# Attention and a squared-ReLU MLP on one core: an h pair ahead of each o stage, weight sums with their tiles taken together

## The chip, the cores and the metric

One core of one Trainium2 chip runs the whole program. Its engines are PE (TensorE, matrix products into PSUM), DVE (VectorE), ACT (ScalarE), POOL (GpSimd) and SP (SyncE, which here only issues transfers). Each engine works through its own queue in order. The time is that of one execution on the device, in microseconds (us); several runs are taken and their median is compared.

## The reference

Causal attention in float32, then an MLP on its output:

```python
# q, k, v: (4, 12, 448, 64); q and k are scaled up by 8
scores = q @ k.transpose / sqrt(64); scores = where(mask, -1e9, scores)
attn = exp(scores - max); attn = attn / (sum + 1e-9)
x = (attn @ v).transpose(0, 2, 1, 3).reshape(1792, 768)
h = maximum(x @ w_in, 0)          # w_in (768, 2048)
out = h * h @ w_out               # w_out (2048, 768); float32 out
```

## The kernel before

**Two halves.** The 1792 tokens are taken in two halves of 896 (two batches each). The first half (up to about 402 us) runs attention for all heads and the MLP of the first 896 tokens. The second half runs the MLP of the other 896 tokens, and this is the part that the change rearranges. Every float32 operand of a product is split into a high part (rounded, type float32r) and a low part (the rest); a product is three matmuls (high x high, high x low, low x high).

**Seven products for eight.** In the second half each 2 x 2 block product is done with seven products of sums of blocks (Strassen's scheme, in Winograd's form); `SEVEN` lists them as 11, 12, s3, s1, s2, 22, s4. The 2048 hidden columns are worked in four groups of 512, in the order `TURNS` = 0, 3, 2, 1. A group `gr` has

- two h pairs (`h_pair`, u = 0 and 1; each 21 products, matmul lines L797, L799, L801). A pair accumulates in four PSUM banks; ACT and DVE move banks into y tiles (pool r, and f_0 to f_2 of late memory), add, apply ReLU and square, and `factor` splits seven results into g7 tiles (high part on POOL or ACT, low part on DVE, line L300). There are 12 g7 tiles (g_92 to g_95, two in each, and g_0 to g_3).
- an o stage (`o_seven`, for the last group `o_last`; 42 or 48 products, lines L922 to L924). Each bank is added into a sum in SBUF (sa, sb) by DVE, or copied by ACT in the first group; some banks are accumulated on again after that.

**Weights of the second half.** A product needs a w tile with both parts; there are nine (eight in `wi`, one named w). Three of the seven can come ready split from DRAM (`wi_split`, lines L737; `wo_split`, L897), which was written in the first half. The sums of weight blocks (s1 to s4) are made by `added_up`: SP loads a block (L672) into an f tile, POOL or ACT negates or copies it (L690, L297), and POOL issues transfers that load another block and add it to the tile (L678). `done` then splits the result into a w tile. Groups 2 and 1 split the plain blocks too (`kept` is false). f tiles: eleven in the `words` buffer of the first half and one in late memory (f_3), shared by the sums (kind oz, up to 12), the x parts (xp), group 0's sums (fz) and the output (tr).

**What sets the order.** Nothing is ordered by hand: each step is an op with a rank (its due time), one or more engines that can do it, and what these cost. `Plan.emit` takes, again and again, the op that can start earliest by these costs (the lower rank where equal), gives it an engine and tiles, and so writes each engine's queue. `w_parts`, `o_parts` and `added_up` give the weight work ranks ahead of its stage by `LEAD` and the numbers in `added_up`; `ahead` and `begun` keep one set of weights behind the one before. `x_part` loads and splits 21 x parts (L660) at the end of the first half.

Of the kernel before, what the change touches and what calls it, by code (L numbers as in the profile page):

```python
# [17 lines left out]
PE, ACT, DVE, POOL, DMA, DMA2 = range(6)  # L18
# [153 lines left out]
def kernel(  # L172
# [17 lines left out]
    nc = tc.nc  # L190
# [35 lines left out]
    TURNS, LEAD = (0, 3, 2, 1), 9  # L226
# [40 lines left out]
    plan.pool("f", [], fz=5, xp=3, oz=12, tr=3)  # L267
# [395 lines left out]
    ahead, begun = [], []  # L663

    def added_up(rank, n, source, done, shaped, kept):

        def loaded(key, at):
            h = Hold("f", "oz")  # L670
            src, saved = source(key)
            plan.op(at, [(DMA, 0.7, lambda: nc.sync.dma_start(out=shaped(h.t[:, :n]), in_=src))],  # L672
                    saved, [h], begun, take=h)
            return h

        def added(h, key, at):
            src, saved = source(key)
            plan.op(at, [(POOL, 1.1, lambda: nc.gpsimd.dma_start(  # L678
                out=shaped(h.t[:, :n]), in_=src, accum_op=ALU.add))], saved, [h])
            plan.op(at, [(DMA, 0.7, lambda: None)], [], [h])  # L680

        def derived(a, scale, h=None, at=0.0, drop=()):
            to, take = (h, None) if h else (Hold("f", "oz"),) * 2

            def dst():
                return to.t[:, :n]

            def src():
                return a.t[:, :n]
            plan.op(at, [(POOL, t_pool(n), lambda: nc.gpsimd.tensor_scalar(  # L690
                dst(), src(), scale, 1.0, op0=ALU.mult, op1=ALU.mult)),
                on_act(n, dst, src, scale=scale)], [a], [to], take=take, drop=drop)
            return to
# [12 lines left out]
        done("s2", b)  # L706
        added(d, "12", rank - 4)
        done("s4", d)
        if not kept:
            done("12", loaded("12", rank - 5))  # L710
            done("22", loaded("22", rank - 3))

    def w_parts(gr, u, rank, last):
# [48 lines left out]
        if gr == 0:  # L762
# [6 lines left out]
            begun[:] = plan.ops[-2:]  # L769
# [14 lines left out]

    def h_pair(u, W, rank, step, plain):

        bank = {k: Hold("ps", "st") for k in "abcd"}
        y = {k: Hold("r", "y") for k in ("u2", "u3", "11", "12", "21")}
        f1, f2 = 2 * u, 2 * u + 1
# [81 lines left out]
        factor("t4", "21", True)  # L871
        return rank
# [7 lines left out]
    g7, sums = {}, {}  # L880
# [49 lines left out]
    def o_seven(gr, W, rank, step):  # L930

        bank = {}
        for key in SEVEN:
            b, k, begin = O_BANK[key], O_SUM[key], key not in ("12", "22", "s4")
            for d in range(CB):
# [3 lines left out]
                rank = o_product(ps, [(W[key, u], g7[OTHER[key], u]) for u in range(2)], d, begin, True, rank, step)  # L939
# [19 lines left out]
    def o_last(W, rank, step):  # L959

        for k in ("11", "21", "12", "22"):
            i, j = k
            for d in range(CB):
                ps, a = Hold("ps", "os"), o_sum(k, d)
                rank = o_product(ps, [(W[i + m, u], g7[m + j, u]) for m in "12" for u in range(2)],
# [68 lines left out]
    def group(ph, gr, rank, step, begin):  # L1034

        if ph == 0:
            for c in range(NP):
                at = begin + (rank - begin) * (c + 0.5) / NP
                piece(at, "i", gr, c, 0, ())
                if gr in (0, NG - 1):  # L1040
                    keep(at + 4, gr, c, swap)
        else:
            us = 7 * CB * H_US * step
            W = [w_parts(gr, u, rank + u * us - LEAD, rank + (u + 1) * us - LEAD) for u in range(2)]
        begin = rank
        if ph == 0 and gr == 0:
# [5 lines left out]
        elif ph == 0:  # L1052
# [3 lines left out]
        else:  # L1056
            for u in range(2):
                rank = h_pair(u, W[u], rank, H_US * step, gr == TURNS[-1])
        if ph == 0:
            for i in range(2 * GF):  # L1060
                at = begin + (rank - begin) * (i + 0.5) / 8
                piece(at, "o", gr, i % GF, i // GF, swap)
            begin = rank
            for ch in range(2):
                for t in range(NT):
                    rank = o_unit(gr, t, ch, rank, O_US * step, swap)
        else:
            begin = rank
            W = o_parts(gr, rank - LEAD, rank + 42 * H_US * step - LEAD)
            rank = o_last(W, rank, H_US * step) if gr == TURNS[-1] else o_seven(gr, W, rank, H_US * step)  # L1070
# [4 lines left out]
    for gr in range(NG):  # L1075
        begin, rank = group(0, gr, rank, (rest + NA * 7.0) / rest, begin)
# [68 lines left out]
```

## Time and profile before

| | |
|---|---|
| median of 3 runs | 628.52 us (626.83 to 628.68) |
| profiled execution | 631.88 us, its span 630.1 us |
| PE busy | 596.7 us, 95% of the span |
| DVE, ACT, POOL busy | 429.3, 358.6, 380.4 us (68%, 57%, 60%) |
| bytes moved | 120.01 MB, mean 190 GB/s |

The profile is of one execution. Busy time is the time in which an engine has an instruction under way; a matmul's duration is longer than its spacing, since matmuls overlap. Times within the span are counted from its start. "Idle before" an instruction is ascribed to what released it. The granted clock is the share of full speed that TensorE's clock was given; 1.00 is 2.4 GHz and 0.50 is 1.2 GHz.

### The profile page before, as it was taken

What the parts mean: (1) busy time and instruction counts of PE and PEld (TensorE: products, weight loads), DVE (VectorE), ACT (ScalarE), POOL (GpSimd) and SP (SyncE); (2) the same over time, 40 slices, a digit from 0 to 9 for tenths busy, and PEclk for the clock granted to TensorE, in tenths of its full rate; (3) what the DMA queues carried; (4) which work ended last, traced back from release to release, by engine and by line L of the source; (5) the groups of instructions that cost most, each with busy time, mean ns of one, the idle gap of its engine ahead of it and who ended that gap; (6) DMA issues with size and microseconds to landing.
All of it is one profiled execution on the core that took longest, in us unless ns stands there. A gap on an engine that the chain in (4) does not pass through costs nothing.

```text
span 630.1 us, 11422 instructions
## 1 busy us (share of the span) xinstructions
PE 596.7 (95%) x3714; PEld 512.8 (81%) x3714; DVE 429.3 (68%) x938; ACT 358.6 (57%) x874; POOL 380.4 (60%) x483
## 2 busy tenths in 40 slices
PE   3979999999999999989999999999899999899996
PEld 2656677789888998778898889998798979799995
DVE  5769866476877878474877327688738944976554
ACT  4679977766776656576456543356455435524510
POOL 1456784568679754778745556468965855576100
PEclk9799999999999999999999999999999989999999
DMA  8987854699988998987996639779697586405555
GB/s 141 172 199 143 156 138 74 139 314 303 237 252 250 254 264 282 241 225 203 235 285 231 221 124 293 246 212 226 131 240 205 109 137 170 114 14 108 155 89 89
DMA packets 203148, 120.01 MB, mean 190 GB/s; under 512 B 138960, under 2 KB 191056, under 8 KB 203088
## 3 DMA queue, kind: packets, MB, share of 16 engines
q1 hardware_dynamic: 181328, 108.01, 62.8%
q0 software_dynamic: 6912, 9.44, 9.9%
q10 hardware_dynamic: 14848, 1.84, 1.9%
q8 instruction: 29, 0.48, 0.3%
q14 instruction: 31, 0.25, 0.1%
HBM read 80.71 MB, written 38.54 MB: 189 GB/s over the span
## 4 chain that ended last, share of the span: by engine, by line
PE 61%; DMA 13%; DVE 11%; ACT 5%; issue 4%; POOL 3%; SPq 3%; ACTq 0%; DVEq 0%; POOLq 0%
PE ps L995 5%; PE ps L432 5%; PE ps L997 5%; PE ps L996 5%; PE ps L922 4%; PE ps L923 4%; PE ps L924 4%; PE ps L620 4%; PE ps L412 4%; PE ps L372 4%; PE ps L801 4%; PE ps L797 4%; PE ps L799 4%; PE ps L621 4%; PE ps L622 4%
## 5 line engine op out<-in xcount | busy, mean ns | idle before, releaser
L297 ACT ACTIVATE words<-words 128x384 f32<-128x384 f32 (+3 forms) x136 | 78.9, 597 | 64.3 <-DMA words<-in_moe_w_out_dram 17.2
L398 POOL TENSOR_SCALAR ap<-ap,asm 128x128 f32<-128x128 f32 (+6 forms) x122 | 76.9, 650 | 47.2 <-DVE asm L457 30.3
L385 DVE CUSTOM_DVE_ANT_0 ps<-ps,mask 128x448 f32<-128x448 f32 (+6 forms) x168 | 68.7, 444 | 20.2 <-PE ps L372 10.8
L995 PE MATMUL ps<-wo,g 128*128 128x384 f32 x224 | 76.8, 343 | 0.0
L620 PE MATMUL ps<-x,wi 128*128 128x448 f32 x192 | 74.6, 389 | 0.7 <-ACT x L297 0.6
L997 PE MATMUL ps<-wo,g 128*128 128x384 f32 x224 | 75.1, 335 | 0.0
L996 PE MATMUL ps<-wo,g 128*128 128x384 f32 x224 | 75.1, 335 | 0.0
L304 POOL TENSOR_TENSOR wi<-words,wi 128x384 fp32r<-128x384 f32 (+1 forms) x53 | 68.9, 1348 | 3.0 <-ACT wi L297 1.3
L621 PE MATMUL ps<-x,wi 128*128 128x448 f32 x192 | 70.2, 366 | 0.2 <-DVE x L300 0.2
L622 PE MATMUL ps<-x,wi 128*128 128x448 f32 x192 | 70.1, 365 | 0.0
L389 ACT ACTIVATE ap<-ps,mx 128x448 f32<-128x448 f32 (+6 forms) x126 | 58.5, 480 | 19.6 <-DVE mx L385 17.6
L922 PE MATMUL ps<-g,wi 128*128 128x448 f32 x162 | 60.0, 370 | 3.1 <-DVE sa L300 2.3
L923 PE MATMUL ps<-g,wi 128*128 128x448 f32 x162 | 59.8, 369 | 0.2 <-DVE g L300 0.2
L924 PE MATMUL ps<-g,wi 128*128 128x448 f32 x162 | 59.7, 368 | 0.0
L310 POOL TENSOR_SCALAR wi<-words 128x384 fp32r<-128x384 f32 (+1 forms) x44 | 30.7, 700 | 44.4 <-DVE words L584 16.6
L797 PE MATMUL ps<-x,wi 128*128 128x448 f32 x147 | 54.7, 372 | 2.1 <-ACT wi L297 1.3
L801 PE MATMUL ps<-x,wi 128*128 128x448 f32 x147 | 54.6, 372 | 0.2 <-DVE wi L300 0.2
L799 PE MATMUL ps<-x,wi 128*128 128x448 f32 x147 | 54.5, 371 | 0.0
L297 ACT ACTIVATE r<-ps 128x448 f32<-128x448 f32 x60 | 32.5, 543 | 34.6 <-DVE r L499 10.6
L300 DVE CUSTOM_DVE_ANT_0 words<-words 128x768 uint16<-128x768 uint16 (+1 forms) x56 | 43.5, 777 | 11.6 <-ACT words L297 8.5
L412 PE MATMUL ps<-ident,ap 128*128 128x128 f32 x288 | 43.3, 283 | 7.9 <-POOL ap L398 7.3
L297 ACT ACTIVATE apt<-ps 128x512 f32<-128x512 f32 x71 | 38.7, 598 | 14.5 <-PE ps L412 14.4
(134 smaller groups left out, 1468.9 us busy)
## 6 DMA issues: line engine op xcount, KB each, us to landing
words<-in_moe_w_in_dram SPq DMA_DIRECT2D x24, 512.0 KB, 5.6
words<-in_moe_w_out_dram SPq DMA_DIRECT2D x32, 384.0 KB, 4.1
wo_split<-wo SPq DMA_DIRECT2D x26, 384.0 KB, 5.1
wi<-wo_split SPq DMA_DIRECT2D x23, 384.0 KB, 3.7
wo_whole<-words SPq DMA_DIRECT2D x32, 192.0 KB, 4.5
wi_split<-wi SPq DMA_DIRECT2D x24, 256.0 KB, 3.5
v<-in_v_dram SPq DMA_DIRECT2D x24, 192.0 KB, 4.7
wi_whole<-words SPq DMA_DIRECT2D x18, 256.0 KB, 4.5
```

The costliest lines, as they stand in the source:

```text
L297: return (ACT, t_act(n, psum, more), lambda: nc.scalar.activation(dst(), src(), func, **kw))
L620: nc.tensor.matmul(o, w[:, 0], x[:, 0], start=c == 0, stop=False)
L621: nc.tensor.matmul(o, w[:, 0], x[:, 1], start=False, stop=False)
L622: nc.tensor.matmul(o, w[:, 1], x[:, 0], start=False, stop=c == NP - 1)
L797: nc.tensor.matmul(o, w.t[:, 0, c], x[:, 0], start=begin and c == 0, stop=False, skip_group_check=True)
L801: nc.tensor.matmul(o, w.t[:, 1, c], x[:, 0], start=False, stop=c == CB - 1, skip_group_check=True)
L922: nc.tensor.matmul(o, w.t[:, 0, d], g.t[:, 0], start=start, stop=False, skip_group_check=True)
L923: nc.tensor.matmul(o, w.t[:, 0, d], g.t[:, 1], start=False, stop=False, skip_group_check=True)
L924: nc.tensor.matmul(o, w.t[:, 1, d], g.t[:, 0], start=False, stop=stop, skip_group_check=True)
L995: nc.tensor.matmul(res(), g[:, 0], w[:, 0], start=f == 0, stop=False)
L996: nc.tensor.matmul(res(), g[:, 0], w[:, 1], start=False, stop=False)
L997: nc.tensor.matmul(res(), g[:, 1], w[:, 0], start=False, stop=f == GF - 1)
```

## The change

The loop over the second half no longer works group by group. A list of stages puts pair 0 of the next group ahead of a group's o stage, and pair 1 behind it; each stage asks for its own weights. With pairs of two groups alive, g7 is keyed by group too, and a pair's factors wait (`earlier`, `drawn`) for the high half of the last factor of the pair before. `added_up` takes all tiles of a set at once (four, or six where plain blocks are split too) and issues its loads in one step, 24 ranks ahead instead of 16 and less. The later steps get ranks from -20 to -7 instead of -13 to -4. `LEAD` goes from 9 to 15. In the planner's costs an accumulating transfer books 2.4 on a queue of its own (DMA2) where it booked 0.7. The x parts have two f tiles instead of three. What is computed stays the same.

```diff
-    TURNS, LEAD = (0, 3, 2, 1), 9
+    TURNS, LEAD = (0, 3, 2, 1), 15
...
-    plan.pool("f", [], fz=5, xp=3, oz=12, tr=3)
+    plan.pool("f", [], fz=5, xp=2, oz=12, tr=3)
...
     def added_up(rank, n, source, done, shaped, kept):
-        def loaded(key, at):
-            h = Hold("f", "oz")
-            src, saved = source(key)
-            plan.op(at, [(DMA, 0.7, lambda: nc.sync.dma_start(out=shaped(h.t[:, :n]), in_=src))],
-                    saved, [h], begun, take=h)
-            return h
-        def added(h, key, at):
+        hs = [Hold("f", "oz") for _ in range(4 if kept else 6)]
+        b, a, c, d = hs[:4]
+        loads = [("11", b), ("21", a)] + list(zip(("12", "22"), hs[4:]))
+        def load():
+            for key, h in loads:
+                nc.sync.dma_start(out=shaped(h.t[:, :n]), in_=source(key)[0])
+        plan.op(rank - 24, [(DMA, 0.9 * len(loads), load)], [k for key, _ in loads for k in source(key)[1]],
+                [h for _, h in loads], begun, take=tuple(hs))
+        begun[:] = plan.ops[-1:] + small
+        def added(key, h, at):
...
-            plan.op(at, [(DMA, 0.7, lambda: None)], [], [h])
+            plan.op(at, [(DMA2, 2.4, lambda: None)], [], [h])
...
-        b = loaded("11", rank - 16)
-        a = loaded("21", rank - 14)
         if not kept:
             done("11", b, False)
-        derived(b, -1.0, b, rank - 13)
-        added(b, "21", rank - 12)
-        c = derived(b, 1.0, at=rank - 9)
+        derived(b, -1.0, b, rank - 20)
+        added("21", b, rank - 19)
+        added("22", a, rank - 18)
+        done("s1", a)
+        derived(b, 1.0, c, rank - 14)
         done("s3", c)
-        added(a, "22", rank - 8)
-        done("s1", a)
-        added(b, "22", rank - 8)
-        d = derived(b, -1.0, at=rank - 5, drop=[b])
+        added("22", b, rank - 13)
+        derived(b, -1.0, d, rank - 8, [b])
         done("s2", b)
-        added(d, "12", rank - 4)
+        added("12", d, rank - 7)
         done("s4", d)
         if not kept:
-            done("12", loaded("12", rank - 5))
-            done("22", loaded("22", rank - 3))
+            for h, key in zip(hs[4:], ("12", "22")):
+                done(key, h)
...
-            begun[:] = plan.ops[-2:]
+            small[:] = plan.ops[-2:]
...
-    def h_pair(u, W, rank, step, plain):
+    def h_pair(gr, u, W, rank, step, plain):
...
-        f1, f2 = 2 * u, 2 * u + 1
+        earlier = list(drawn)
...
-            g7[key, u] = g = Hold("g7", "g7")
-            split(rank, S, lambda: g.t[:, 0], lambda: g.t[:, 1], lambda: y[k].t, [y[k]], g, (),
+            g7[gr, key, u] = g = Hold("g7", "g7")
+            split(rank, S, lambda: g.t[:, 0], lambda: g.t[:, 1], lambda: y[k].t, [y[k]], g, earlier,
...
         factor("t4", "21", True)
+        drawn[:] = plan.ops[-2:-1]
         return rank
...
-    for ph in range(1, NPH):
-        for gr in TURNS:
-            begin, rank = group(ph, gr, rank, 1.0, begin)
+    stages = [(TURNS[0], 0), (TURNS[0], 1)]
+    for n, gr in enumerate(TURNS):
+        after = TURNS[n + 1:n + 2]
+        stages += [(a, 0) for a in after] + [(gr, None)] + [(a, 1) for a in after]
+    for gr, u in stages:
+        last = gr == TURNS[-1]
+        if u is None:
+            W = o_parts(gr, rank - LEAD, rank + 42 * H_US - LEAD)
+            rank = o_last(W, rank, H_US) if last else o_seven(gr, W, rank, H_US)
+        else:
+            W = w_parts(gr, u, rank - LEAD, rank + 7 * CB * H_US - LEAD)
+            rank = h_pair(gr, u, W, rank, H_US, last)
```

The queues that come out of it differ from the second half on, and on SP, POOL, ACT and DVE from the last attention steps of the first half. Three places:

PE's queue before, where the last product of group 0's second pair ends (x_90 is its last x part) and the o stage begins:

```order
L797 MATMUL ps_120<-x_90,wi 128x448
L799 MATMUL ps_120<-x_90,wi 128x448
L801 MATMUL ps_120<-x_90,wi 128x448
L922 MATMUL ps_115<-g_92,wi 128x448
L923 MATMUL ps_115<-g_92,wi 128x448
L924 MATMUL ps_115<-g_92,wi 128x448
```

and now (x_3 to x_5 are the x parts of product 12, here of pair 0 of group 3):

```order
L797 MATMUL ps_120<-x_90,w_4249 128x448
L799 MATMUL ps_120<-x_90,w_4249 128x448
L801 MATMUL ps_120<-x_90,w_4249 128x448
L797 MATMUL ps_115<-x_3_3938,wi 128x448
L799 MATMUL ps_115<-x_3_3938,wi 128x448
L801 MATMUL ps_115<-x_3_3938,wi 128x448
```

The first product of the o stage (L923 to L925 now) stands 12 products further on (three of that pair's products stand ahead of these rows), and o products alternate with the rest of the pair.

DVE's queue before, at the start of group 2's o stage (sa are the first three sums; g are low halves of factors of its second pair, r and f its y tiles):

```order
L300 TENSOR_TENSOR g_92<-r_98,g_92 128x448
L300 TENSOR_TENSOR r_102<-r_102,r_98 128x448
L300 TENSOR_TENSOR g_94<-r_100,g_94 128x448
L300 TENSOR_TENSOR r_97<-r_97,r_102 128x448
L300 TENSOR_TENSOR g_92<-r_102,g_92 128x448
L300 TENSOR_TENSOR g_93<-f_1_4201,g_93 128x448
L300 TENSOR_TENSOR g_95<-r_97,g_95 128x448
L300 TENSOR_TENSOR g_2_4197<-f_2_4202,g_2_4197 128x448
L300 TENSOR_TENSOR r_101<-r_99,r_101 128x448
L300 TENSOR_TENSOR sa_3936<-ps_116,sa_3936 128x448
L300 TENSOR_TENSOR sa_3937<-ps_117,sa_3937 128x448
L300 TENSOR_TENSOR sa_3938<-ps_114,sa_3938 128x448
```

and now, at the same three sums (the pair just before is pair 0 of group 1):

```order
L300 TENSOR_TENSOR g_92<-r_101,g_92 128x448
L300 TENSOR_TENSOR f_0_4250<-ps_116,f_0_4250 128x448
L300 TENSOR_TENSOR f_2_4252<-ps_120,f_2_4252 128x448
L300 TENSOR_TENSOR r_98<-ps_118,r_102 128x448
L300 TENSOR_TENSOR f_0_4250<-f_0_4250,f_2_4252 128x448
L300 TENSOR_TENSOR r_97<-ps_113,f_2_4252 128x448
L300 TENSOR_TENSOR r_100<-r_98,r_100 128x448
L300 TENSOR_TENSOR sa_3944<-ps_117,sa_3944 128x448
L300 TENSOR_TENSOR sa_3945<-ps_114,sa_3945 128x448
L300 TENSOR_TENSOR sa_3946<-ps_119,sa_3946 128x448
```

The sums moved ahead of most of the factors.

SP's queue before, from the loads of group 3's o weights on (L672 loads a block for a sum, L737 and L897 load ready w tiles):

```order
L672 DMA words<-wi_whole 128x384
L897 DMA wi<-wo_split 128x768 x4
L897 DMA w_4199<-wo_split 128x768
L672 DMA words<-wi_whole 128x384
L672 DMA words<-wo_whole 128x384
L897 DMA wi<-wo_split 128x768
L672 DMA words<-wo_whole 128x384
L672 DMA words<-wi_whole 128x384
```

and now (L676 loads the blocks of a set, L898 is L897 of before):

```order
L676 DMA words<-wo_whole 128x384 x4
L898 DMA wi<-wo_split 128x768 x6
L676 DMA words<-wi_whole 128x384 x8
L676 DMA words<-wo_whole 128x384 x2
L898 DMA w_4249<-wo_split 128x768
L898 DMA wi<-wo_split 128x768 x3
```

The single loads that alternated with ready tiles became sets of two and four.

## Rows read from the trace of the kernel before

**Rows 1.** Windows: span, busy time (count) per engine, clock, DMA share, GB/s.

```profile
402.70:428.40 25.70, 25.70 (x128) 23.69 (x127) 18.78 (x31) 13.14 (x27) 13.00 (x17) 1.00 0.81 226
428.40:457.90 29.50, 26.75 (x127) 23.23 (x126) 22.11 (x24) 17.87 (x38) 27.81 (x31) 1.00 0.82 177
457.90:484.80 26.90, 26.06 (x128) 23.59 (x127) 16.51 (x24) 13.78 (x28) 15.11 (x19) 1.00 0.95 235
484.80:510.40 25.60, 25.60 (x128) 23.71 (x128) 22.19 (x35) 12.14 (x24) 16.92 (x21) 1.00 0.57 112
510.40:539.80 29.40, 27.91 (x128) 24.82 (x127) 13.15 (x21) 15.19 (x31) 18.67 (x23) 0.94 0.75 162
539.80:569.80 30.00, 27.74 (x127) 24.86 (x126) 25.56 (x41) 10.24 (x19) 20.05 (x23) 0.94 0.22 49
569.80:597.90 28.10, 28.10 (x139) 25.90 (x139) 16.00 (x27) 15.11 (x29) 9.83 (x13) 1.00 0.58 144
597.90:625.30 27.40, 26.96 (x134) 24.64 (x132) 15.39 (x25) 1.74 (x3) 0.00 (x0) 1.00 0.55 89
```

**Rows 2.** Timeline of PE: start, duration, instruction, idle before it and its releaser.

```profile
448.33 0.47 PE L923 MATMUL ps<-g,w 128*128 128x448 f32 x1 [1.73 <-DVE g L300]
...
482.95 0.44 PE L797 MATMUL ps<-x,wi 128*128 128x448 f32 x1 [0.84 <-DVE r L300]
...
513.64 0.47 PE L797 MATMUL ps<-x,wi 128*128 128x448 f32 x1 [1.25 <-ACT wi L297]
...
548.39 0.47 PE L922 MATMUL ps<-g,wi 128*128 128x448 f32 x1 [2.26 <-DVE sa L300]
```

**Rows 3.** Windows behind two of these waits, columns as in rows 1.

```profile
515.40:519.00 3.60, 3.60 (x12) 3.19 (x11) 0.00 (x0) 0.77 (x2) 2.11 (x3) 0.53 1.01 173
...
549.50:553.20 3.70, 3.70 (x12) 3.32 (x11) 3.64 (x7) 0.79 (x2) 0.05 (x1) 0.54 0.02 4
```

**Rows 4.** Timeline of DVE ahead of the waits at 448.33 and 548.39.

```profile
441.65 6.62 DVE L300 TENSOR_TENSOR g<-f,g 128x448 fp32r<-128x448 f32 x2 [0.46 <-POOL g L310]
...
547.73 1.67 DVE L300 TENSOR_TENSOR sa<-ps,sa 128x448 f32<-128x448 f32 x3
```

**Rows 5.** Timeline of POOL while the two instructions of 441.65 ran.

```profile
444.26 2.58 POOL L304 TENSOR_TENSOR wi<-words,wi 128x384 fp32r<-128x384 f32 x2
...
446.80 3.29 POOL L304 TENSOR_TENSOR wi<-words,wi 128x384 fp32r<-128x384 f32 x2
```

**Rows 6.** Timeline of ACT and POOL ahead of the wait at 513.64.

```profile
512.24 0.94 ACT L297 ACTIVATE words<-words 128x384 f32<-128x384 f32 x2 [4.57 <-POOL w L304]
513.08 0.92 ACT L297 ACTIVATE wi<-words 128x384 fp32r<-128x384 f32 x2
...
508.55 0.86 POOL L678 DMA_DIRECT2D words<-wo_whole  x1 [4.52 <-DMA words<-wo_whole]
```

**Rows 7.** Groups from 400 us on: busy us, mean ns, idle before, releasers.

```profile
L300 DVE TENSOR_TENSOR g<-r,g 128x448 fp32r<-128x448 f32 x34 | 23.7, 702 | 10.5 <-ACT g L297 6.8 <-POOL g L310 3.6
...
L300 DVE TENSOR_TENSOR wi<-words,wi 128x384 fp32r<-128x384 f32 x25 | 14.4, 594 | 7.7 <-ACT wi L297 7.3 <-POOL wi L310 0.4
...
L690 POOL TENSOR_SCALAR words<-words 128x384 f32<-128x384 f32 x8 | 5.4, 669 | 2.1 <-DVE wi L300 1.2 <-DMA words<-wi_whole 0.8
```

**Rows 8.** DMA issues, 402 to 620 us: count, KB each, median us to landing.

```profile
words<-wo_whole POOLq DMA_DIRECT2D x22, 192.0 KB, 6.2
words<-wi_whole POOLq DMA_DIRECT2D x22, 192.0 KB, 4.5
words<-wi_whole SPq DMA_DIRECT2D x18, 192.0 KB, 3.9
```

**Rows 9.** Timeline of SP's last x load, and of ACT.

```profile
400.49 0.38 SPq L660 DMA_DIRECT2D words<-x_dram  x1
...
373.79 0.98 ACT L297 ACTIVATE r<-ps 128x448 f32<-128x448 f32 x2 [4.95 <-DVE r L499]
...
403.10 0.58 ACT L297 ACTIVATE x<-words 128x448 fp32r<-128x448 f32 x1 [2.19 <-DMA words<-x_dram]
```

More of the change, by code (lines that the diff above doesn't have):

```diff
@@ L661, in x_part @@
         split(rank, S, lambda: t()[:, 0], lambda: t()[:, 1], lambda: h.t, [h], ("x7", key, i), [after], [h])
-    ahead, begun = [], []
+    ahead, begun, small = [], [], []
     def added_up(rank, n, source, done, shaped, kept):
-        def loaded(key, at):
-            h = Hold("f", "oz")
-            src, saved = source(key)
-            plan.op(at, [(DMA, 0.7, lambda: nc.sync.dma_start(out=shaped(h.t[:, :n]), in_=src))],
-                    saved, [h], begun, take=h)
-            return h
-        def added(h, key, at):
+        hs = [Hold("f", "oz") for _ in range(4 if kept else 6)]
[8 more added lines that the diff above has]
+        def added(key, h, at):
             src, saved = source(key)
@@ L679, in added, with derived @@
                 out=shaped(h.t[:, :n]), in_=src, accum_op=ALU.add))], saved, [h])
-            plan.op(at, [(DMA, 0.7, lambda: None)], [], [h])
-        def derived(a, scale, h=None, at=0.0, drop=()):
-            to, take = (h, None) if h else (Hold("f", "oz"),) * 2
+            plan.op(at, [(DMA2, 2.4, lambda: None)], [], [h])
+        def derived(a, scale, h, at, drop=()):
             def dst():
-                return to.t[:, :n]
+                return h.t[:, :n]
             def src():
@@ L879 @@
     O_SUM = {"11": "u2", "12": "11", "s3": "22", "s1": "22", "s2": "u2", "22": "21", "s4": "12"}
-    g7, sums = {}, {}
+    g7, drawn = {}, []
     def o_parts(gr, rank, last):
@@ L938, in o_seven @@
                 ps = bank[b, d]
-                rank = o_product(ps, [(W[key, u], g7[OTHER[key], u]) for u in range(2)], d, begin, True, rank, step)
+                rank = o_product(ps, [(W[key, u], g7[gr, OTHER[key], u]) for u in range(2)], d, begin, True, rank, step)
                 def src(ps=ps):
@@ L964, in o_last @@
                 ps, a = Hold("ps", "os"), o_sum(k, d)
-                rank = o_product(ps, [(W[i + m, u], g7[m + j, u]) for m in "12" for u in range(2)],
+                rank = o_product(ps, [(W[i + m, u], g7[TURNS[-1], m + j, u]) for m in "12" for u in range(2)],
                                  d, True, True, rank, step)
@@ L1032, with group @@
     swap = [plan.op(0.0, [(DMA, 0.0, enter)], after=list(plan.ops))]
[L1034 to L1044, printed above, removed]
+    def group(gr, rank, step, begin):
+        for c in range(NP):
+            at = begin + (rank - begin) * (c + 0.5) / NP
+            piece(at, "i", gr, c, 0, ())
+            if gr in (0, NG - 1):
+                keep(at + 4, gr, c, swap)
         begin = rank
-        if ph == 0 and gr == 0:
+        if gr == 0:
             r = NP * PAIR + 16
@@ L1051, in group @@
                 rank = h_unit(f, 1, rank, H_US * step)
-        elif ph == 0:
+        else:
             for f in range(GF):
@@ L1055, in group @@
                     rank = h_unit(f, h, rank, H_US * step)
[L1056 to L1070, printed above, removed]
+        for i in range(2 * GF):
+            at = begin + (rank - begin) * (i + 0.5) / 8
+            piece(at, "o", gr, i % GF, i // GF, swap)
+        begin = rank
+        for ch in range(2):
+            for t in range(NT):
+                rank = o_unit(gr, t, ch, rank, O_US * step, swap)
         return begin, rank
@@ L1075 @@
     for gr in range(NG):
-        begin, rank = group(0, gr, rank, (rest + NA * 7.0) / rest, begin)
+        begin, rank = group(gr, rank, (rest + NA * 7.0) / rest, begin)
     mark = len(plan.ops)
```

4 lines of the change are left out of this document (2 added, 2 removed).

## The prediction

> **What bounds the kernel now.** I read the stretches of the second half first [rows 1]. Stage names: h(3) is the h stage of group 3, h(3,0) its first pair, o(3) its o stage; the order before is h(0), o(0), h(3), o(3), h(2), o(2), h(1), o(1). In the stretches of h(0) and o(3) PE is busy without a break: 25.70 and 25.60 us for 126 matmuls each (42 products of three), so 25.65 us is the undisturbed price of such a stage, 0.2036 us a matmul. The excess over it is what scheduling can still give: o(0) 29.50 - 25.65 = 3.85, h(3) 1.25, h(2) 3.75, o(2) 4.35. h(1) and o(1) together take 55.5 us for 270 matmuls, 55.0 at that price: 0.5. Sum 13.7 us of a span of 630.1. PE is the bound; the other engines have room on average (DVE at most 25.56 of 30.0 us, in o(2)). Before 402.7 the change moves no matmul, so that part stays.
>
> The timeline of PE says what each excess is [rows 2]. In o(0) the longest wait is 1.73 us for the low half of a factor on DVE. In h(3) it waits 0.84 us for a DVE addition. In h(2) it waits 1.25 us for a weight tile's high half on ACT. In o(2) it waits 2.26 us for a DVE addition into a sum, which must read a bank before PE accumulates on in it. After the last two the granted clock falls: 0.53 over 3.60 us and 0.54 over 3.70 us [rows 3], most of each stretch at the lower level of 1.2 GHz; that costs (1 - 0.53) x 3.60 = 1.7 us each. It didn't fall after the 1.73 us. So h(2) is 1.25 + 1.7 and a rest of small waits, o(2) is 2.26 + 1.7 and a rest.
>
> Then I read the engines that were waited for.
> - DVE before 448.3: two low halves of factors take 6.62 us together [rows 4], though one takes 0.70 us in the mean where it reads an r tile [rows 7]. POOL runs subtractions of weight parts meanwhile, four of them in 5.87 us from 444.26 [rows 5]; both engines' instructions have two inputs in SBUF.
> - DVE before 548.4: it comes to o(2)'s first sums at 547.73 [rows 4], 8 us into the stage; its order shows h(2,1)'s factors ahead of them.
> - ACT before 513.1: it stood still until 512.24 for a negation that is a step of a weight sum, and the two high halves that PE needs stood behind it at 513.08 [rows 6]. POOL in turn had waited 4.52 us for a landing. So an in-order queue was held by a later set's sum.
>
> **The change, part by part.**
> 1. *A pair ahead of the o stage.* Products, additions, factors and sums are all as many as before; PE's matmuls stay 1026 in the second half. Before, o(0) began right behind h(0,1)'s last product; now 15 of h(3,0)'s 21 products, 15 x 3 x 0.2036 = 9.2 us, stand ahead of o(0)'s first, and the other six are mixed into its beginning. The waits of o(0) are for factors of h(0,1). They had to come within o(0)'s first 20 us; they now have 9.2 us more at least, against a lateness of 1.73. What hides them is h(3,0). I take 2.8 of o(0)'s 3.85: 1.73 and part of the small waits around it; 1.0 stays, since the o stage is now mixed with a pair. Bounds: 0 and 3.85.
> 2. *DVE's queue at o(2).* Its order shows what stood ahead of o(2)'s first three sums: nine instructions on factors and y tiles in a row, none of which reads a bank. Of the seven ahead of them now, four are additions that read a bank, as PE needs them. 2.26 us and its clock loss should go: I take 3.3 of 4.35. Bounds: 0 (two pairs still stand side by side ahead of every o stage but the last, as h(3,1) and h(2,0), so DVE has the same burst) and 4.35.
> 3. *The sums.* All loads of a set now go out together and 39 ranks ahead (lead 15 and 24) where the first went 25 ahead (9 and 16). The planner also books 2.4 for an accumulating transfer on a separate queue where it booked 0.7. In the trace such a transfer takes 4.5 us (h parts) to 6.2 us (o parts) from issue to landing, a load 3.9 [rows 8]. Three accumulations stand in a row: 3.9 + 3 x 5.35 + 3 negations or copies of 0.67 [rows 7] = 22 us a set. The order before packed instructions behind steps that landed later than booked, which is the wait of h(2). I take all of its 3.75. Bounds: 0 and 3.75.
> 4. *h(3)'s 1.25.* The wait is inside a pair: PE accumulates in a bank that DVE must have read. Nothing in the change touches that: 0 gained.
> 5. *New cost.* Pairs are mixed with o stages in four places, so such a wait can come up where o sums and a pair's additions share DVE. Not shown in the trace; the nearest row is h(3)'s 1.25 with one in a stage. Bounds: 0 and four of them, 5.0; I take 1.5 of them, 1.8 us.
> 6. *POOL and DVE.* The planner gives some ten subtractions more to DVE and as many fewer to POOL: 10 x 0.6 us [rows 7], spread over the 222.6 us from 402.7 to 625.3, of which DVE is busy 150 (the eight stretches of [rows 1] added): nothing on the path.
> 7. *Only two x parts at a time, and the first loads of group 3's sums in SP's queue ahead of them.* Before, the last x load was issued at 400.49 and its high half made at 403.10 [rows 9]; it is used in the seventh product group of h(0,0), 18 products or 11 us behind 402.7. A tile less delays the chain by about one load, 3.9 us: hidden by those 11 us, and up to 2 us if that cover is used up. I take 0. The steps that POOL and ACT now run for these sums stand between the last attention's instructions; ACT stood idle for 4.95 us until 373.79 there [rows 9], which hides them. If that cover were gone, a split of PE's factors would come late by one POOL transfer, about 1 us.
>
> Sum: 2.8 + 3.3 + 3.75 - 1.8 = 8.0 us. The profiled execution took 631.88 us (span 630.1), 3.4 above the median of the runs; so 623.9 for it, and **628.5 - 8.0 = 620.5 us** for the median. All parts at their best: 13.2 us, 615.3.
>
> **A page against a row.** Where the low halves took 3.3 us each, the trace shows DVE slowed while POOL subtracted [rows 4, 5]. The Trainium skill, "SBUF — State Buffer", section "Who interferes with whom", says that a DVE instruction with two inputs in SBUF and a GpSimd instruction that reads SBUF exclude each other for the whole instruction. The trace agrees in kind, but by the page one wait would be one POOL instruction (1.3 us here), and the rows show about 2.7 us of waiting per instruction. By that rule a new order moves the clashes and doesn't remove them; that is the third rival below.
>
> **The rivals.**
> - *Only the sums' wait goes.* DVE's bursts stay, since two pairs still follow each other and its factors cost what they did. Gained: 3.75, so 624.8 us. For it: DVE was busy 25.56 us of o(2)'s 30.0 [rows 1]. Against it: the order of DVE at o(2).
> - *Slower: the tiles of the sums.* There are 12 f tiles; a set now takes its 4 or 6 at once and early. The 12 sets take 56 tiles. One held for 22 us of chain and one pair's stage, 35 us in all, makes 56 x 35 / 12 = 163 us of the roughly 180 us from 402.7 to the last pair at 583 (569.8 and half a stage). It decides from a hold of 38.6 us (180 x 12 / 56), that is landings of 5.35 + 3.8 / 3 = 6.6 us in the mean; the o parts' 6.2 are near that. Then weights come late in three later stages (h(1,0), o(2), h(1,1)) as in h(2) now: 620.5 + 3 x 3.75 = 631.8 us. Against it: loads that start before 402.7 give more room.
> - *No change: the stalls move.* POOL and DVE meet elsewhere, and waits like h(3)'s come up in all the four mixed places with one clock fall: 5.0 + 1.7 instead of 1.8, and o(0)'s wait (2.8) stays as a clash elsewhere: 620.5 + 4.9 + 2.8 = 628.2.
>
> **How the numbers follow.** Forecast 60%, its own range 616 to 624; only the sums 17%; no change 11%; slower 12%. About 0.3%, 1.9 us, is what a measurement of this kernel can tell from nothing. The first two cases are faster (77%). The range for eight in ten takes the forecast and the second case and some of the third: 616 to 628.5; 615.3 bounds it below.
>
> **What the profile after would show.** Right: o(0)'s first product stands about 9 us later, without a wait for a g tile; no wait of PE for an ACT or DVE weight part at the start of h(2); the clock stays at 1.00 from 402.7 to 625; POOL's waits for landings shrink. Wrong: PE waits for wi or w tiles in h(1,0), o(2) or h(1,1) (tiles of the sums); PE waits for DVE additions in the mixed places; a low half on DVE again takes 3 us or more; a wait in the first product groups of h(0,0) for an x part.

## The result, and the profile after

The changed kernel takes **618.6 us** (median of 4 runs, 617.64 to 619.18), the one before 628.31 us beside it (4 runs, 626.83 to 628.68). The ratio is 0.9848, with a 95% interval of 0.9827 to 0.987, so it is faster by 1.3 to 1.7%. The forecast was 620.5 us.

The profiled execution took 618.13 us with a span of 616.4. The windows of the second half, cut where the stages now begin (o(0)'s first product stands at 434.65, o(3)'s at 488.38; columns as in [rows 1]):

```profile
399.65:434.65 35.00, 34.99 (x171) 31.84 (x170) 28.23 (x47) 23.72 (x47) 15.83 (x20) 1.00 0.83 223
434.65:464.53 29.88, 29.42 (x146) 26.97 (x144) 22.55 (x32) 17.53 (x36) 20.47 (x23) 1.00 0.52 139
488.38:516.69 28.31, 27.77 (x137) 25.27 (x136) 26.27 (x39) 12.51 (x25) 18.23 (x23) 1.00 0.40 87
541.18:568.15 26.97, 26.97 (x134) 24.71 (x133) 26.68 (x38) 12.68 (x26) 17.87 (x20) 1.00 0.42 93
```

PE is busy through all of them and the granted clock is 1.00, where [rows 1] had 0.94 in h(2) and o(2). DVE is full in o(2) (26.68 of 26.97 us), and PE does not wait for it there.

PE's timeline: the first and last matmul of the second half, and between them the only two waits that are left.

```profile
399.45 0.37 PE L797 MATMUL ps<-x,wi 128*128 128x448 f32 x1
...
439.52 0.44 PE L797 MATMUL ps<-x,wi 128*128 128x448 f32 x1 [0.46 <-DVE r L300]
...
509.15 0.47 PE L923 MATMUL ps<-g,wi 128*128 128x448 f32 x1 [0.54 <-DVE sa L300]
...
609.97 0.36 PE L925 MATMUL ps<-g,wi 128*128 128x448 f32 x1
```

The same two ends in the trace of the kernel before, for the length of its second half:

```profile
402.74 0.37 PE L797 MATMUL ps<-x,wi 128*128 128x448 f32 x1
...
624.50 0.36 PE L924 MATMUL ps<-g,wi 128*128 128x448 f32 x1
```

From the first to the last start there are 1025 steps of 0.2036 us, 208.7 us. The kernel before took 221.76 us for them and lost 13.1; the changed one took 210.52 and lost 1.8. So the second half gained 11.3 us between these two executions. The first half began it 3.3 us earlier, with nothing changed on PE; over all the profiles of this study that start lies between 399.45 and 403.76 us (in g4 that of its fourth matmul; three stand at 391.61, among the first half's), so this is taken as scatter, as is the place of the profiled run of before (3.6 us above its median). By the medians the gain is 9.7 us.

What changed little is seen in the groups from 400 us on (columns as in [rows 7]) and in the landings (those of SP's own loads are shorter, 2.7 us against 3.9 in [rows 8]):

```profile
L300 DVE TENSOR_TENSOR g<-r,g 128x448 fp32r<-128x448 f32 x38 | 27.2, 729 | 12.4 <-ACT g L297 10.5 <-POOL g L310 1.9
L300 DVE TENSOR_TENSOR wi<-words,wi 128x384 fp32r<-128x384 f32 x26 | 19.4, 770 | 6.7 <-POOL wi L310 4.1 <-ACT wi L297 2.6
L300 DVE TENSOR_TENSOR g<-f,g 128x448 fp32r<-128x448 f32 x12 | 15.0, 1266 | 2.8 <-POOL g L310 2.7
...
L304 POOL TENSOR_TENSOR wi<-words,wi 128x384 fp32r<-128x384 f32 x23 | 27.1, 1221 | 3.5 <-ACT wi L297 3.2
```

```profile
words<-wo_whole POOLq DMA_DIRECT2D x22, 192.0 KB, 5.5
words<-wi_whole POOLq DMA_DIRECT2D x18, 192.0 KB, 4.6
words<-wi_whole SPq DMA_DIRECT2D x17, 192.0 KB, 2.7
```

DVE's low halves are no quicker than in [rows 7] (g<-r 729 ns against 702, wi<-words 770 against 594; g<-f 1266 against 1355). An undisturbed one takes 0.61 us (448 columns) or 0.55 us (384), the medians of those beside which POOL runs nothing. Taking that off every DVE instruction with both inputs in SBUF, over the second half, leaves 22.5 us of waiting before and 25.6 us after. Of this 15.9 and 22.1 us stand beside POOL's two-input instructions, 6.5 and 3.4 us beside its one-input copies and negations, and 0.1 us where POOL has no such work. So the clashes of DVE with POOL, of which [rows 4, 5] show one, cost DVE no less than they did. They now fall where PE can go on. One stands in o(2), on DVE and POOL:

```profile
550.28 4.42 DVE L300 TENSOR_TENSOR g<-f,g 128x448 fp32r<-128x448 f32 x2
554.62 3.80 DVE L300 TENSOR_TENSOR sb<-ps,sb 128x448 f32<-128x448 f32 x7
...
551.25 1.01 POOL L304 TENSOR_TENSOR wi<-f,wi 128x384 fp32r<-128x384 f32 x1
552.23 1.01 POOL L304 TENSOR_TENSOR w<-words,w 128x384 fp32r<-128x384 f32 x1
553.21 1.01 POOL L304 TENSOR_TENSOR wi<-words,wi 128x384 fp32r<-128x384 f32 x1
```

DVE loses over 3 us, then adds seven sums in a row, and PE never stops.

### The profile page after: what moved, and what is told of

Its sections match the earlier page's. It is cut to its first block, busy times and chain, and to the rows that moved or that the text cites. A ratio compares the mean times of both kernels' runs of the same rounds, so it can differ in the third digit from the quotient of the medians.

```text
span 616.4 us, 11415 instructions
## 1 busy us (share of the span) xinstructions
PE 591.6 (96%) x3714; PEld 510.4 (83%) x3714; DVE 433.8 (70%) x950; ACT 360.8 (59%) x882; POOL 356.8 (58%) x463
## 4 chain that ended last, share of the span: by engine, by line
PE 66%; DMA 10%; DVE 9%; POOL 5%; issue 3%; ACT 3%; SPq 2%; ACTq 0%; DVEq 0%; POOLq 0%
PE ps L923 6%; PE ps L925 6%; PE ps L924 6%; PE ps L996 5%; PE ps L432 5%; PE ps L998 5%; PE ps L997 5%; PE ps L412 4%; PE ps L372 4%; PE ps L797 4%; PE ps L801 4%; PE ps L620 4%; PE ps L799 4%; PE ps L621 3%; PE ps L622 3%
## 5 line engine op out<-in xcount | busy, mean ns | idle before, releaser
L385 DVE CUSTOM_DVE_ANT_0 ps<-ps,mask 128x448 f32<-128x448 f32 (+6 forms) x168 | 68.6, 443 | 20.1 <-PE ps L372 11.5
L304 POOL TENSOR_TENSOR wi<-words,wi 128x384 fp32r<-128x384 f32 (+1 forms) x44 | 54.9, 1270 | 4.8 <-ACT wi L297 3.2
L923 PE MATMUL ps<-g,wi 128*128 128x448 f32 x156 | 57.1, 366 | 0.5 <-DVE sa L300 0.5
L924 PE MATMUL ps<-g,wi 128*128 128x448 f32 x156 | 57.0, 366 | 0.0
L925 PE MATMUL ps<-g,wi 128*128 128x448 f32 x156 | 57.0, 365 | 0.0
L300 DVE CUSTOM_DVE_ANT_0 words<-words 128x768 uint16<-128x768 uint16 (+1 forms) x56 | 43.2, 772 | 11.3 <-ACT words L297 8.0
L581 DVE TENSOR_SCALAR words<-words 128x384 int32<-128x384 int32 (+1 forms) x56 | 29.5, 531 | 25.0 <-ACT words L297 24.8
```

Source lines behind the costliest of these rows:

```text
L923: nc.tensor.matmul(o, w.t[:, 0, d], g.t[:, 0], start=start, stop=False, skip_group_check=True)
L924: nc.tensor.matmul(o, w.t[:, 0, d], g.t[:, 1], start=False, stop=False, skip_group_check=True)
L925: nc.tensor.matmul(o, w.t[:, 1, d], g.t[:, 0], start=False, stop=stop, skip_group_check=True)
```

## The experiments

Four theories were set against each other. *The terms add*: the order takes away o(0)'s and o(2)'s waits, the sums h(2)'s. *A*: it takes the order and early sums together. *B*: the written queues react to any number, and the changed kernel is a lucky one among its neighbours. *C*: what the kernels lose is above all DVE held up by POOL's subtractions. In the table, "lost" is PE's time in the second half beyond 208.7 us, "waits" the part of it that PE's timeline names, "clash" DVE's time beyond the undisturbed one as above; these three are of the profiled execution. In e3, g1 and g4 that is the fastest run and in g3 the slowest, so there they are not those of a median run.

| kernel | median us (runs) | ratio [95%] | profiled run | lost | waits | clash |
|---|---|---|---|---|---|---|
| before | 628.31 (4) | 1 | 631.88 | 13.1 | 7.3 | 22.5 |
| changed | 618.6 (4) | 0.9848 [0.9827, 0.987] | 618.13 | 1.8 | 1.0 | 25.6 |
| e1 order alone | 631.18 (12) | 1.0036 [1.0007, 1.0065] | 631.28 | 13.5 | 8.7 | 22.6 |
| e2 sums alone | 636.26 (6) | 1.0119 [1.0078, 1.0159] | 636.85 | 18.5 | 12.0 | 27.3 |
| e3 booking alone | 641.57 (6) | 1.0231 [1.0183, 1.0278] | 639.84 | 23.9 | 16.7 | 20.1 |
| e4 changed, old booking | 625.11 (12) | 0.9956 [0.9931, 0.9982] | 624.57 | 6.3 | 3.9 | 27.8 |
| f1 changed, lead 18 | 624.77 (11) | 0.9919 [0.9891, 0.9947] | 625.67 | 6.1 | 3.5 | 27.7 |
| f2 changed, lead 12 | 623.89 (12) | 0.9931 [0.99, 0.9961] | 623.08 | 5.8 | 4.5 | 32.3 |
| f3 changed, 10 tiles | 627.88 (12) | 0.9983 [0.9961, 1.0005] | 626.66 | 9.3 | 5.7 | 33.1 |
| f4 changed, single tiles | 630.26 (12) | 1.0022 [0.9992, 1.0051] | 628.53 | 11.8 | 8.0 | 25.2 |
| g1 changed, no POOL subtractions | 621.14 (6) | 0.989 [0.9848, 0.9932] | 618.99 | 2.8 | 1.6 | 11.3 |
| g2 g1 with lead 12 | 620.06 (6) | 0.9857 [0.982, 0.9893] | 620.13 | 2.3 | 0.8 | 11.0 |
| g3 before, no POOL subtractions | 621.27 (7) | 0.9895 [0.9858, 0.9932] | 626.28 | 6.5 | 4.0 | 12.7 |
| g4 order and lead 15, old sums | 633.02 (12) | 1.008 [1.0045, 1.0115] | 628.08 | 12.0 | 9.3 | 25.1 |

Each ratio is against the kernel before on the same chip (its medians there: 628.31 beside the changed kernel, 628.51 for e, 628.70 for f, 629.01 for g). It is formed from the single runs and so is not exactly the quotient of the medians. The 12.0 of g4 counts from its fourth matmul on.

**e1, the new order alone.** The kernel before with the parts of the diff in the stages, in h_pair and in o_seven; its sums, lead and bookings stay.

```diff
+    stages = [(TURNS[0], 0), (TURNS[0], 1)]
...
+        stages += [(a, 0) for a in after] + [(gr, None)] + [(a, 1) for a in after]
```

> The new order of stages alone, with the old sums (tiles one by one, lead 9, the old booking of an accumulating transfer, three x tiles). Theory (the terms add): the waits of o(0) and o(2) go with the order, h(2)'s wait for a weight part stays: 618.6 + 3.75 = 622.4 us, with a wait of PE for a weight part (ACT or DVE, wi or w) of about 1.3 us and a fall of the clock. Rival (the sums carry all): the order alone brings little, 626 to 629 us, since weights come late in more than one stage.

631.18 us: no gain, a little slower, which neither expectation had. PE's three longest waits, ACT ahead of the first of them, and one clash of DVE and POOL ahead of the third (timeline):

```profile
442.71 0.44 PE L797 MATMUL ps<-x,wi 128*128 128x448 f32 x1 [4.11 <-ACT words L297]
467.57 0.74 PE L923 MATMUL ps<-g,w 128*128 128x448 f32 x1 [2.40 <-DVE sa L300]
524.38 0.47 PE L923 MATMUL ps<-g,wi 128*128 128x448 f32 x1 [1.47 <-DVE sa L300]
...
438.55 0.52 ACT L297 ACTIVATE wi<-words 128x384 fp32r<-128x384 f32 x1 [2.47 <-DMA words<-wi_whole]
442.11 0.52 ACT L297 ACTIVATE words<-words 128x384 f32<-128x384 f32 x1 [2.58 <-issue]
...
518.23 3.97 DVE L300 TENSOR_TENSOR r<-r,r 128x448 f32<-128x448 f32 x1
...
518.45 3.25 POOL L304 TENSOR_TENSOR wi<-words,wi 128x384 fp32r<-128x384 f32 x3
```

The waits for factors in o(0) are gone, as step 1 said. A weight part of h(3,0) is late instead: ACT stands 2.47 us for a landing of a sum, and another 2.58 us for nothing that the profile names, before the copy that PE is said to wait for. And waits for DVE's additions (sa) are there, in o(0) and o(3).

**e2, the sums alone.** The kernel before with the new added_up, its bookings, lead 15 and two x tiles; the order of stages stays.

```diff
-    TURNS, LEAD = (0, 3, 2, 1), 9
+    TURNS, LEAD = (0, 3, 2, 1), 15
...
+        plan.op(rank - 24, [(DMA, 0.9 * len(loads), load)], [k for key, _ in loads for k in source(key)[1]],
+                [h for _, h in loads], begun, take=tuple(hs))
```

> The new sums alone (a set's tiles together, lead 15, the longer booking, two x tiles) in the old order of stages. Theory (the terms add): h(2)'s 3.75 us go, the waits of o(0) and o(2) for DVE stay: 628.3 - 3.75 = 624.6 us, with PE waits for DVE of about 1.7 and 2.3 us at o(0) and o(2). Rival (the sums carry all): 619 to 620 us without those waits. Second rival (tiles are short in the old order): 630 us or more.

636.26 us, slower. That is in the range of the rival that tiles are short, but no weight part is late any more, so that wait is what the sums are good for. But two long waits stand in o(0) and o(2) (timeline of PE, then of DVE and POOL ahead of them):

```profile
448.79 0.74 PE L923 MATMUL ps<-g,wi 128*128 128x448 f32 x1 [3.17 <-DVE g L300]
553.38 0.47 PE L922 MATMUL ps<-g,wi 128*128 128x448 f32 x1 [3.82 <-DVE sa L300]
...
443.39 4.80 DVE L300 TENSOR_TENSOR f<-f,f 128x448 f32<-128x448 f32 x1
546.94 4.79 DVE L300 TENSOR_TENSOR f<-f,r 128x448 f32<-128x448 f32 x1
...
444.51 3.20 POOL L304 TENSOR_TENSOR wi<-words,wi 128x384 fp32r<-128x384 f32 x3
```

One DVE addition, 0.61 us when undisturbed, takes 4.80 us: it ends at 448.19, 0.5 us behind the last of POOL's three subtractions (447.71). PE's factor stands behind it on DVE.

**e3, the booking alone.** The kernel before with one number of the planner.

```diff
-            plan.op(at, [(DMA, 0.7, lambda: None)], [], [h])
+            plan.op(at, [(DMA2, 2.4, lambda: None)], [], [h])
```

> The kernel before with one number changed: an accumulating transfer is booked with 2.4 on a queue of its own. Theory (the old order packed instructions behind steps that land later than booked): the ACT wait of 4.57 us ahead of h(2) shrinks and with it PE's wait: 624.6 us. Rival (only the longer lead helps, a booking alone merely shuffles): 627 to 631 us.

641.57 us: a booking nearer to the landings of [rows 8] costs 13 us, which neither expectation had. PE's main waits by line and releaser (total, times, longest):

```profile
PE ps L923 <- DVE g L300: 4.9, 5, 1.5
PE ps L922 <- ACT g L297: 3.2, 4, 1.1
PE ps L922 <- DVE f L300: 3.1, 1, 3.1
PE ps L924 <- POOL wi L304: 2.5, 1, 2.5
```

All are in o stages, and most are for factors (g). With the longer booking the planner writes o(2)'s first products ahead of h(2,1)'s last 45 matmuls (by the timeline of PE o(2) begins behind 333 h matmuls; in the kernel before, behind all 378 of h(0), h(3) and h(2)). So o(2) comes closer to the factors that it needs.

**e4, the changed kernel with the old booking.** The same line, turned back in the changed kernel.

> The changed kernel with the old booking of 0.7 for an accumulating transfer. Theory: the lead of 39 ranks covers three landings of 5 us each whatever is booked: 618.6 to 619.6 us. Rival (the booking is what removed h(2)'s wait): about 622 us, with ACT or POOL waiting 4 us and more for a landing and PE for a weight part.

625.11 us: some 6.5 us slower than the changed one, so the booking counts there too, with the other sign. It was not expected so: the longest wait for a weight part is 0.27 us. Its longest wait (the next, of 0.94 and 0.89 us, are for ACT):

```profile
499.31 0.47 PE L923 MATMUL ps<-g,wi 128*128 128x448 f32 x1 [1.33 <-DVE sa L300]
```

After e1 to e4 "the terms add" has fallen: the order is worth -2.7, the sums with their numbers -7.8, and both together +9.7. The next four kernels change numbers of the changed kernel, or how its tiles are taken.

**f1 and f2, the lead.**

```diff
-    TURNS, LEAD = (0, 3, 2, 1), 15
+    TURNS, LEAD = (0, 3, 2, 1), 18
```

f2 has 12 in the same place.

> The changed kernel with the lead of the weight parts at 18 ranks instead of 15; nothing else differs. Theory A (the gain comes from the order of stages together with sums that are made early; the lead only has to be long enough): 617.5 to 621 us, and PE's waits from 402 us to the end stay under 3 us in all. Theory B (the queues that are written are sensitive to any number, and 618.6 is a lucky draw among them): the time lands anywhere between 620 and 634 us, as the four kernels with parts of the change did (625.1 to 641.6), with new waits of 1 to 4 us at places that differ from one kernel to the next.

> The changed kernel with the lead of the weight parts at 12 ranks instead of 15. Theory A: 617.5 to 621 us if 12 ranks are long enough; if they are too short, one wait of PE for a weight part stands at the start of a pair (1 to 4 us, as the 4.11 us for words of h(2,0) in the kernel that has the order alone), so 620 to 623, and the waits have ACT or POOL weight parts as their cause and no others. Theory B: 620 to 634 us, with waits for factors and additions of DVE as well.

624.77 and 623.89 us. Neither a longer nor a shorter lead keeps the whole gain, and no weight part is late in f2. (The 4.11 us of e1 that f2's expectation names are for a part of h(3,0), not h(2,0), by the count of matmuls ahead.) f1's main wait is 2.75 us for DVE sa in o(2). f2's two waits stand there too, and this is what DVE and POOL did ahead of the second:

```profile
551.06 0.47 PE L923 MATMUL ps<-g,wi 128*128 128x448 f32 x1 [1.69 <-DVE sa L300]
556.18 0.47 PE L923 MATMUL ps<-g,wi 128*128 128x448 f32 x1 [2.42 <-DVE sa L300]
...
551.46 4.13 DVE L300 TENSOR_TENSOR g<-r,g 128x448 fp32r<-128x448 f32 x1
...
550.90 4.19 POOL L304 TENSOR_TENSOR wi<-words,wi 128x384 fp32r<-128x384 f32 x4
```

The addition sa that PE needs is next in DVE's queue and starts at 555.51, when the held factor ends. It is a clash like the changed kernel's at 550.28, which PE rode out.

**f3, ten tiles for the sums.**

```diff
-    plan.pool("f", [], fz=5, xp=2, oz=12, tr=3)
+    plan.pool("f", [], fz=5, xp=2, oz=10, tr=3)
```

> The changed kernel with 10 f tiles for the sums' parts instead of 12. The prediction's slower rival: a set takes its 4 or 6 tiles together, and a set that has to wait for them makes its weights late. If tiles are nearly short at 12 (that rival's mechanism, from 56 tiles for 12 sets), 10 give waits of PE for wi or w parts in h(1,0), o(2) or h(1,1), 3.75 us each: 622 to 630 us. If a set holds its tiles for well under 30 us, 10 cost nothing that PE sees: 618 to 620 us. Theory B, that any change of a number moves the time: 620 to 634 us, but the waits are then not for weight parts.

627.88 us, inside that rival's range, but not by its mechanism:

```profile
484.19 0.44 PE L797 MATMUL ps<-x,w 128*128 128x448 f32 x1 [0.92 <-POOL words L693]
563.49 0.74 PE L923 MATMUL ps<-g,wi 128*128 128x448 f32 x1 [4.58 <-DVE sb L300]
...
555.02 7.35 DVE L300 TENSOR_TENSOR g<-r,g 128x448 fp32r<-128x448 f32 x2
...
556.92 4.50 POOL L304 TENSOR_TENSOR wi<-words,wi 128x384 fp32r<-128x384 f32 x4
```

One wait of 0.92 us is for a weight sum. The 4.58 us are for a DVE addition behind two factors that took 7.35 us; the second of them ran beside four subtractions in a row on POOL.

**f4, tiles taken singly.** Order, lead, bookings and the ranks of the steps on POOL and ACT as in the changed kernel; each tile is taken by the step that fills it first, and the loads of 12 and 22 go out at their own rank.

```diff
-        plan.op(rank - 24, [(DMA, 0.9 * len(loads), load)], [k for key, _ in loads for k in source(key)[1]],
-                [h for _, h in loads], begun, take=tuple(hs))
+        loaded("11", b, rank - 24)
+        loaded("21", a, rank - 24)
...
+                loaded(key, h, rank - 13)
```

> The changed kernel, in which each f tile of a set is taken by the step that first fills it (the two first loads 24 ranks ahead, the loads of 12 and 22 and the copy 13 to 14 ahead, the last negation 8 ahead), and not all together; order of stages, lead, the order of the sums' steps and bookings are those of the changed kernel. If taking together matters in itself (a set that has begun never waits for a tile in its middle, with queues behind it): 621 to 626 us, with a wait for weight parts at the start of a pair. If it is only a way to write the same thing: 617.5 to 620.5 us. Theory B: anywhere from 620 to 634 us.

630.26 us: the whole gain is gone. PE's waits here are for loads of ready tiles and for factors:

```profile
438.97 0.47 PE L924 MATMUL ps<-g,wi 128*128 128x448 f32 x1 [1.05 <-DMA wi<-wo_split]
441.82 0.44 PE L924 MATMUL ps<-g,wi 128*128 128x448 f32 x1 [1.36 <-DMA wi<-wo_split]
558.58 0.47 PE L924 MATMUL ps<-g,w 128*128 128x448 f32 x1 [1.60 <-ACT g L297]
```

They are not the late weight sums that were expected if taking together mattered in itself; the ready tiles of o(0) come late through SP's queue. So theory A, in which only order and earliness count, fails in f1, f2 and f4. B describes them, but says nothing of a cause; the clashes in e1, e2, f2 and f3 led to C.

**g1, g2 and g3, no subtractions of weights on POOL.** One line, in the changed kernel (g1), in f2 (g2) and in the kernel before (g3). The low halves of both h and o weights are then made on DVE alone.

```diff
-    HWAY, OWAY, GWAY = slice(None), slice(1, 2), slice(0, 1)
+    HWAY, OWAY, GWAY = slice(0, 1), slice(0, 1), slice(0, 1)
```

> The changed kernel, in which all low halves of the second half's weights (h and o) are subtracted on DVE and none on POOL; copies and negations stay free to go to POOL. Theory C (what the kernels near the changed one lose, 4 to 10 us, is mostly DVE factors held up while POOL runs several subtractions in a row, as 7.35 us for two g<-r,g beside 4.50 us of four POOL subtractions with 10 f tiles, and 4.13 us for one beside 4.19 us of four with a lead of 12): no two-input DVE instruction takes over 2 us from 402 us on, and PE waits less than 2 us: 617 to 620 us. Rival (DVE's own load bounds: some 29 subtractions more at 0.55 us are 16 us on an engine that is busy for 150 of 210 us): waits of PE for DVE sa, sb or g tiles of 1 to 3 us in the o stages, 621 to 627 us.

> As the kernel before it, with the lead at 12 ranks. With POOL's subtractions the lead of 12 cost 5.3 us against 15 (623.89 to 618.6), in two waits for DVE sa of 1.69 and 2.42 us. Theory C: without them it costs nothing, 617 to 620 us, within 1.5 us of the kernel with 15. Rival (DVE's load): 621 to 628. Theory B (any number moves the queues, whatever the clashes): 3 us or more away from the kernel with 15, to either side.

> The kernel before, with all low halves of the second half's weights on DVE. Theory C: of its 7.3 us of waits the one for DVE sa (2.26) and the one for DVE g (1.73) with their clock falls go, so 622 to 625 us; the two for ACT wi (1.25) and DVE r (0.84) stay. Rival (those waits are of the old order of stages itself, with DVE's bursts at the start of an o stage): 627 to 632 us, with waits for DVE g and sa at the first products of o(0) and o(2) still there or longer, since DVE has 16 us more to do.

621.14, 620.06 and 621.27 us. The group rows of g1 on DVE, from 400 us on:

```profile
L300 DVE TENSOR_TENSOR wi<-words,wi 128x384 fp32r<-128x384 f32 x53 | 30.8, 591 | 10.2 <-ACT wi L297 9.1 <-POOL wi L310 1.1
L300 DVE TENSOR_TENSOR g<-f,g 128x448 fp32r<-128x448 f32 x12 | 8.5, 705 | 3.6 <-ACT g L297 2.0 <-POOL g L310 1.6
```

DVE makes 53 of these low halves instead of 26, and each at 591 ns, near the undisturbed 0.55; g<-f falls from 1266 to 705 ns. Clash time falls from 25.6 to 11.3 us (8.6 of them now beside POOL's copies), which nearly pays for the 29 more subtractions (29 x 0.55 = 16 us). g1's time lies 1.1 us above what theory C had and just inside the range of the rival, DVE's load. But its one wait for DVE sa is 0.7 us, so in the profiled run, its fastest, that load hardly bound; g2 lies 1.1 us from g1, as C had it. The lead, which had cost 5.3 us between 15 and 12, makes no measurable difference any more (1.1 us, and the intervals of g1 and g2 overlap). And the kernel *before*, with old order and old sums, gains 7.7 us by this one line (6.6 by the ratio): 621.27 us, a little more than C had. Its waits for DVE sa and for weights are gone. The longest left are these, and behind the second, in o(2), the granted clock is 0.53 over 3.6 us:

```profile
PE ps L797 <- ACT r L297: 1.9, 1, 1.9
PE ps L923 <- DVE g L300: 0.8, 1, 0.8
```

**g4, the new order with lead 15 and the old sums.**

> The new order of stages and the lead of 15 ranks, with the old sums (single tiles, order and bookings of before). Tells whether the order needs the new sums or only parts that start earlier. If the lead alone does it: the wait of 4.11 us for words of h(2,0), which the order with the lead of 9 had, is gone, and the time is that of the kernels near the changed one, 622 to 626 us. If the new sums are needed: weight parts still come late at the start of a pair (waits of 2 us or more for ACT or POOL parts), 628 to 634 us.

633.02 us, so a longer lead without the new sums does not help the order. (The wait of e1 named in this expectation is that of h(3,0) again.) The time is in the range of late weight parts, but the longest wait is for DVE; the next, 2.12 us, is for the landing of a ready w tile. A clash makes 3.5 of the 5.99 us (4.13 against 0.61):

```profile
442.80 0.71 PE L797 MATMUL ps<-x,wi 128*128 128x448 f32 x1 [5.99 <-DVE r L300]
...
437.99 4.13 DVE L300 TENSOR_TENSOR r<-r,f 128x448 f32<-128x448 f32 x1
...
438.44 3.19 POOL L304 TENSOR_TENSOR wi<-words,wi 128x384 fp32r<-128x384 f32 x3
```

## Why the prediction was right, and where it was not

The time (620.5 against 618.6) and the range held. Point by point:

- *Step 1, o(0).* Right in place and a little small in size. o(0)'s first product stands 35.2 us behind the first of h(0) where it stood 25.7: 9.5 us later, where 9.2 was worked out. No wait for a factor is left there, nor in o(0) of any of the nine other kernels with the new order. The profile gives nearly all of the 3.85 us, where 2.8 was taken.
- *Step 2, o(2).* Right for the changed kernel (all of 4.35, 3.3 taken), not enough as a reason. The wait for DVE sa was put down to the order of DVE's queue. With the new order it comes back in e1 (in o(0) and o(3)), f1 and f2, and as sb in f3; in e1, f2 and f3 a DVE instruction held beside POOL's subtractions stands ahead of it. In the trace of the kernel before, DVE works without a break from 538.65 to the sums at 547.73, and five instructions there take 2.7 us more than undisturbed, the first row below among them: the clashes alone come to as much as the wait of 2.26 us. The order may count too. In g3, with the old order of stages, the wait goes, but the planner also wrote the first of o(2)'s sums ahead of a row of factors (second row), so g3 does not part the two.
- *Step 3, the sums.* h(2)'s 3.75 us is gone, and no kernel with the new sums but f3 (0.92 us) waits over 0.4 us for a weight part that is summed. But taken alone they cost 7.8 us, and the booking alone 13.
- *Step 4, h(3).* "0 gained" was too low: PE's only wait in h(3) is now the 0.46 us that step 5 counts too. The 13.2 us of "all parts at their best" hold the whole 1.25 of h(3), for which this step names no gain.
- *Step 5, new cost.* 1.8 us taken, 1.0 found: the waits of 0.46 us, where h(3,0) and o(0) are mixed, and of 0.54 us, in o(3) some 16 us behind its last mixed product (o(3) runs alone from 492.64).
- *Steps 6 and 7, costed at nothing.* POOL subtracts 29 weight parts instead of 36, some seven fewer where ten were taken, and PE waits for no x part. In e2, f1 and f4, which have two x tiles as well, it waits 0.57 us for one, within the bound of 2 us.
- *A reading.* The low halves of [rows 4] did not take 3.3 us each: the first took 0.62 us, the second 6.08. So not 2.7 us per instruction were waited there but 5.5 by one.

```profile
538.65 1.41 DVE L300 TENSOR_TENSOR r<-r,r 128x448 f32<-128x448 f32 x1
...
532.82 0.62 DVE L300 TENSOR_TENSOR sa<-ps,sa 128x448 f32<-128x448 f32 x1 [1.20 <-PE ps L924]
...
442.19 6.08 DVE L300 TENSOR_TENSOR g<-f,g 128x448 fp32r<-128x448 f32 x1
```

The first and the third row are of the kernel before, the second of g3.

The sum, 8.0 us, came near the measured 9.7. **The step that failed is the addition itself.** Steps 1 to 3 were each priced as the removal of a wait with a cause of its own. By that the order alone would have given 622.4 us and the sums alone 624.6; e1 and e2 measured 631.18 and 636.26. What the runs showed in its place: the parts share DVE and POOL, and where a low half meets a row of subtractions is set by all of the planner's numbers together. That the sum came out near the measured gain is in part luck: with the same order and the same way of taking tiles, e4, f1, f2 and f3 gain 3.4, 3.9, 4.8 and 0.8 us.

The third rival, that the stalls move, had 11% and had the mechanism. The clash time did not fall (22.5 us before, 25.6 after), as that rival had it. What it missed is that a clash costs only where PE has nothing ahead of it, so moving them can be worth much of the difference. Without POOL's subtractions the old order and the new take the same time within their intervals (621.27 and 621.14), which speaks for the order and the sums bringing mostly cover from clashes. That is argued and not shown: the one line also takes work off POOL (busy for 87.6 us of g3's second half where it was 121.4 before, 82.2 in g1 where it was 105.5) and changes the written queues as any number does, and no run parts these. Where a trace shows the chain, in e2, f2 and f3, it is a held DVE instruction that PE's wait goes back to. The other two rivals fell: o(2)'s and o(0)'s waits went with the sums', and tiles were not short (landings of 5.5 us for o parts where 6.2 was feared, and 0.92 us of waiting even with ten tiles).

What stays open: whether lead 15 with this booking meets PE's slack by chance or for a reason. Five neighbours (e4, f1 to f4) lie 5.3 to 11.7 us above it, which speaks for chance, but each of them also changes something real. The changed kernel, g1, g2 and g3 were not run on one chip together; the intervals of their ratios overlap with its own, so none of them is shown to beat it or to fall behind it.

## What to carry to other kernels

When the time depends on queues that a planner writes, the terms of a change do not add: run each part alone, and shift one or two numbers that should not matter, before a gain is put down to a cause. Read not only what PE waits for but how long the instruction that it waits for took against its undisturbed time: here 0.61 us against 4 to 5 us named the cause at once. One line that nearly halves the clash time (no subtractions of weights on POOL) was worth 7.7 us to the old kernel, most of what the whole change brought.

## What the hardware showed that was not expected

A DVE instruction with two inputs in SBUF was held not for one POOL instruction but for a row of them. By start and duration it ended at 522.20 in e1, POOL's three subtractions at 521.70; in e2 at 448.19 and 447.71; in f2 at 555.59 and 555.09; in g4 at 442.12 and 441.63: each time 0.5 us behind the end of the row, near its own undisturbed 0.61 us. In [rows 4, 5] DVE came in while POOL's row went on (448.27 against 450.09), so this is not always so. The Trainium skill, "SBUF — State Buffer", section "Who interferes with whom", speaks of an exclusive lock on the shared ports and of contention between such a DVE instruction and a POOL instruction that reads SBUF; the lock agrees with these rows, the row of several instructions goes beyond what it states.
